# Transposes of one row chunk moved from TensorE to the DMA engines, with a reordered start and a split last tile

## The chip, the cores and the metric

The kernel runs on one NeuronCore of a Trainium2 chip. The metric is device time in microseconds (us); lower is better. Each kernel was run several times, each time beside runs of the kernel before on the same chip. The page and the traces come from the hardware profiler; their time zero is the start of the span, which is about 2 us shorter than the device time.

Engines are named as in the profile: PE is TensorE (matmuls), PEld its weight loads, DVE VectorE, ACT ScalarE, POOL GpSimd, SP SyncE. A "q" behind a name means the queue from which that engine issues DMA transfers. PSUM is the memory that PE writes to; the program has a pool `psum` of eight buffers of 128 x 512 f32 in it, called banks here.

## The reference, cut to what matters

```python
x = A_x                                          # [1, 2048, 1024] bf16
h = x + _A_ref(_layernorm(x), A_wqkv, A_wo)      # dilated local attention, 32 heads of 32
return h + _B_ref(_layernorm(h), B_w_gate, B_w_up, B_w_down)   # (x@w_gate * x@w_up) @ w_down
```

LayerNorm has no learned scale. `A_wqkv` is 1024 x 3072.

## The kernel before

The 2048 rows are worked through in four chunks of 512, each chunk in four tiles of 128 rows. A tile is normalized on DVE (`ln`, rows on partitions) and transposed (`lnT`, features on partitions), the layout in which PE's products here read it. The query-key-value product of a chunk is 24 groups of 8 matmuls. Each group fills one PSUM bank, which ScalarE copies to `sg`, and SyncE stores `sg` to DRAM in the layout that the attention reads back.

Chunk 0's transposes are on PE at the very start. Chunk 1's are on PE too, between matmul groups of chunk 0. Those of the other chunks are DMA transposes issued by SyncE.

```python
def stats(src, mv4, t):                   # DVE
    ...bn_stats of two halves, bn_aggr
def rstd_of(mv4, rs4, lo, hi):            # ScalarE: rs = exp(-0.5 ln(var + eps))
    nc.scalar.activation(rs4[:, lo:hi], mv4[:, lo:hi, 1], ACTF.Ln, bias=eps[:])
    nc.scalar.activation(rs4[:, lo:hi], rs4[:, lo:hi], ACTF.Exp, scale=-0.5)
...
    def transpose(self, t):
        ...
        nc.sync.dma_start_transpose(lnTs[c][:, :, bass.ts(t, 128)], self.lns[t][:])
    def transpose_on_array(self, t):
        ...
        for hf in range(2):
            pt = psum.tile([128, KO // 2, 128], BF, tag="mm", name=f"ptb{c}_{t}_{hf}")
            for kk in range(KO // 2):
                nc.tensor.transpose(pt[:, kk, :], self.lns[t][:, bass.ts(4 * hf + kk, 128)], ident[:])
            copy = nc.vector.tensor_copy if hf else nc.scalar.copy
            copy(lnTs[c][:, bass.ts(hf, 4), bass.ts(t, 128)], pt[:])
...
def evac_qkv(c, m, ps):
    sg = t1k.tile(...)
    nc.scalar.copy(sg[:, HB:HB + TC], ps[:])      # frees the bank of group m
    ...nc.sync.dma_start(<qd, kd or vd in DRAM>, <sg>)
...
qkv(0, range(1, 4))
load_qk(0)                                # GpSimd reads queries and keys of chunk 0 back (qD, kD)
bg.finish(rows2)
for t in range(4):
    norm1[2].transpose(t)                 # SyncE
xtiles[3] = load_x(3, "x", nc.sync)       # four 256 KB loads, SyncE
pump(6)
bg.add(stats_gen(norm1[3]), bg.now + 6.0) # statistics of chunk 3, 6 us later by the kernel's own count
start_attention(0)
qkv(1, range(4))
```

Work added to `bg` is emitted between matmul groups, by an estimate of time that the program keeps; so the *order* of instructions in each engine's queue is fixed when the kernel is built.

Of the kernel before, what the change touches and what calls it, by code (L numbers as in the profile page):

```python
# [78 lines left out]
def kernel(  # L79
# [11 lines left out]
    nc = tc.nc  # L91
# [114 lines left out]
    lnTs = {}  # L206
# [3 lines left out]
    class Norm1:  # L210
# [11 lines left out]
        def norm(self, t):  # L222
            self.lns[t] = normalize(xtiles[self.c][t], self.mv4, self.rs4, t)

        def transpose(self, t):
            c = self.c
            if c not in lnTs:
                lnTs[c] = lnTp.tile([128, KO, TC], BF, tag="lnT", name=f"lnT1_{c}")
            nc.sync.dma_start_transpose(lnTs[c][:, :, bass.ts(t, 128)], self.lns[t][:])

        def transpose_on_array(self, t):
            c = self.c
# [9 lines left out]
    def rows_gen(n, on_array):  # L242
        for t in range(6):
            if t < 4:
                n.stat(t)
                yield 1.5
            if 0 < t < 5:
                n.norm(t - 1)
                yield 0.55
            if t > 1 and on_array:  # L250
                n.transpose_on_array(t - 2)
                yield 0.45

    def stats_gen(n):
        for t in range(4):
# [16 lines left out]
    def load_x0(t):  # L272
        nc.sync.dma_start(x0[t][:], x[bass.ds(t * 128, 128), :])

    def load_w0(lo, n):
        nc.scalar.dma_start(w0[:, lo:lo + n, :], wqkv_v[:, lo:lo + n, 0:512])

    load_w0(0, 4)
    load_w0(4, 4)
    for t in range(4):  # L280
        load_x0(t)
    nc.scalar.preload_act_table_set("natural_log_exp_and_others")
    warm = t1k.tile([128, TC], BF, tag="t1k", name="warm")
    nc.vector.memset(warm[:], 0.0)
    eps = const.tile([128, 1], F32)
# [39 lines left out]
    def first_half(t, i):  # L325
        if i == 0:
            sts[t] = small.tile([128, 2, nc.vector.BN_STATS_DIM], F32, tag="st", name=f"st0_{t}")
        nc.vector.bn_stats(out=sts[t][:, i, :], in_=x0[t][:, bass.ts(i, 512)])

    def first_rstd(t):  # L330
        nc.vector.bn_aggr(out=mv0[:, t, :], in_=sts[t][:])
        rstd_of(mv0, rs0, t, t + 1)
# [3 lines left out]
    def first_norm(t):  # L336
        lns[t] = lnp.tile([128, D], BF, tag="ln", name=f"ln0_{t}")
        for i in range(2):
            cols = bass.ts(i, 512)
            nc.vector.tensor_scalar(lns[t][:, cols], x0[t][:, cols], mv0[:, t, 0:1], rs0[:, t:t + 1],  # L340
                                    ALU.subtract, ALU.mult)

    def first_transpose(t):
        for hf in range(2):
            pt = psum.tile([128, KO // 2, 128], BF, tag="mm", name=f"pt{t}_{hf}")
            for kk in range(KO // 2):
                nc.tensor.transpose(pt[:, kk, :], lns[t][:, bass.ts(4 * hf + kk, 128)], ident[:])
            nc.scalar.copy(lnTs[0][:, bass.ts(hf, 4), bass.ts(t, 128)], pt[:])

    def first_mm(t, kos):  # L350
        for ko in kos:
            for j in range(4):
                nc.tensor.matmul(ps0[j][:, bass.ts(t, 128)], lhsT=wts["qkv", 0][:, ko, bass.ts(j, 128)],  # L353
                                 rhs=lnTs[0][:, ko, bass.ts(t, 128)], start=(ko == 0), stop=(ko == KO - 1))
# [3 lines left out]
    first_half(0, 1)  # L358
    first_rstd(0)
    for t in range(4):  # L360
        if t < 3:
            first_half(t + 1, 0)
        first_norm(t)
        if t < 3:
            first_half(t + 1, 1)
        if t > 0:
            first_mm(t - 1, range(0, 6))
        first_transpose(t)
        if t > 0:
            first_mm(t - 1, range(6, 8))  # L370
        if t < 3:
            first_rstd(t + 1)
# [6 lines left out]
    xtiles[2] = load_x(2, "x", nc.sync)  # L379
    norm1 = {c: Norm1(c) for c in (1, 2, 3)}  # L380
    bg.add(rows_gen(norm1[1], True))
    rows2 = rows_gen(norm1[2], False)
    bg.add(rows2)
    for j in range(4):
# [374 lines left out]
    def f16(ap):  # L759
        return ap.bitcast(F16)  # L760
# [19 lines left out]
    def fcells(homes):  # L780
        return [f16(t[:, k, :]) for t in homes for k in range(NH)]

    def dprod(ps, q, lhs, rhs, fresh, lo=0, n=TC):
        for k in range(NP):
            nc.tensor.matmul(ps[:, bass.ds(lo, n)], lhsT=lhs[k][:, bass.ts(q, 128)], rhs=rhs[k][:, bass.ds(lo, n)],  # L785
                             start=(fresh and k == 0), stop=(k == NP - 1), skip_group_check=not fresh)

    def result(c, rows, t, hf, ps, sc, other, lo=0, n=TC):
        cols = bass.ds(hf * 512 + lo, n)
        nc.vector.scalar_tensor_tensor(rows[:, cols], ps[:, bass.ds(lo, n)], sc,  # L790
                                       rows[:, cols] if other is None else other[:, bass.ds(lo, n)], ALU.mult, ALU.add)
        nc.sync.dma_start(outf[bass.ds(c * TC + t * 128, 128), cols], rows[:, cols])
# [124 lines left out]
    hs2 = hss[2]  # L917
# [83 lines left out]
    down = {}  # L1001
# [28 lines left out]
    ps_x = [psum.tile([128, TC], F32, tag="mm", name=f"dx{q}") for q in range(4)]  # L1030
    ps_y = [psum.tile([128, TC], F32, tag="mm", name=f"dy{q}") for q in range(4)]
# [6 lines left out]
    for q in range(4):  # L1038
        dprod(ps_x[q], q, HA["11"], fcells(down["b11"]), True)
        if q == 1:  # L1040
            scale_h.total(ps_y[3])
            inv = const.tile([128, 1], F32, name="inv_hd")
            nc.vector.tensor_tensor(inv[:], scale_h.inv, scale_d.inv, ALU.mult)
            inv = inv[:]
# [3 lines left out]
    HF = {k: [f16(a) for a in HA[k]] for k in HA}  # L1048
# [17 lines left out]
    p5 = []  # L1066
# [21 lines left out]
    for q in range(4):  # L1088
        dprod(ps_x[q], q, HF["22"], fcells(down["b21"]), False)
        result(3, hs3[q], q, 0, ps_x[q], inv, None)  # L1090
    for q, lo, n in ((0, 0, 512), (1, 0, 512), (2, 0, 512), (3, 0, 256), (3, 256, 256)):
        dprod(ps_y[q], q, HF["12"], fcells(down["b22"]), False, lo, n)
        result(2, hs2[q], q, 1, ps_y[q], inv, p5[q], lo, n)


# [1 line left out]
_INS = ['A_x', 'A_wqkv', 'A_wo', 'B_x', 'B_w_gate', 'B_w_up', 'B_w_down']  # L1097
# [26 lines left out]
```

## Time and profile before

| what | value | from |
|---|---|---|
| time, median | 780.2 us (779.8 to 780.3, four runs) | runs beside the changed kernel |
| PE busy | 770.7 of 778.0 us | page, busy times |
| sum of PE's waits | 3.9 us, six entries | view of waits |
| `ptb` transposes on PE | 32, 1.79 us | chain of waits |
| x of chunk 3, first tile landed | 54.43 us | the trace's record of issues and landings |

The lines behind the rows stand in the prediction. To read the page: "busy" is time in which an engine has an instruction at work; the chain runs back from the last instruction, at each step to what released it.

### The profile page before, as it was taken

To read this page: it belongs to the slowest core of one execution; us is meant where nothing else is said; L and a number is where in the kernel's file an instruction comes from. 1 tells how busy PE (TensorE), PEld (TensorE's weight loads), DVE (VectorE), ACT (ScalarE), POOL (GpSimd) and SP (SyncE) were. 2 spreads that over 40 slices of the span, in tenths; PEclk is the share of its full clock that TensorE was granted. 3 is DMA by queue.
4 is the path that set the end of the run, shared out by engine and by line. 5 is a ranking of instruction groups with operands and counts; after the bars stand their busy time and mean duration, and the time that the engine had idled before them with its cause. 6 is when DMAs were issued, how large, how long until landed. Compare 5 with 4: busy or idle time off the path is not lost.

```text
span 778.0 us, 10494 instructions
## 1 busy us (share of the span) xinstructions
PE 770.7 (99%) x3707; PEld 355.2 (46%) x3707; DVE 614.8 (79%) x805; ACT 473.3 (61%) x1028; POOL 142.1 (18%) x152
## 2 busy tenths in 40 slices
PE   8999999999999999999999999999999999999997
PEld 6544444444444444444444444444444444444444
DVE  6619999999899998999989989985554444579762
ACT  4626544323576652966769799746777677788230
POOL 0000000010000200002000001008778677600000
PEclk9999999999999999999999999999999999999999
DMA  8999693895955869867645383734332323730001
GB/s 279 254 230 209 166 286 84 259 297 144 341 191 169 298 206 237 276 208 247 219 155 196 115 308 107 168 91 115 101 106 58 109 72 92 260 119 28 1 27 55
DMA packets 181605, 133.86 MB, mean 172 GB/s; under 512 B 79024, under 2 KB 174384, under 8 KB 179504
## 3 DMA queue, kind: packets, MB, share of 16 engines
q1 hardware_dynamic: 176912, 110.12, 49.6%
q0 software_dynamic: 3584, 22.02, 8.2%
q10 hardware_dynamic: 1056, 1.05, 0.4%
q8 instruction: 29, 0.48, 0.3%
q14 instruction: 24, 0.20, 0.1%
HBM read 104.86 MB, written 22.02 MB: 163 GB/s over the span
## 4 chain that ended last, share of the span: by engine, by line
PE 89%; DVE 9%; DMA 1%; issue 0%; ACT 0%; SPq 0%; DVEq 0%
PE ps L390 20%; PE pu L390 12%; PE pg L390 12%; PE dx L785 6%; PE pz L678 6%; PE acc L624 6%; PE py L678 6%; PE px L678 6%; PE wo L511 4%; PE pv L678 3%; PE dy L785 3%; DVE h L832 1%; PE ps L353 1%; PE ex L785 1%; DVE h L790 1%; DVE prodx L778 1%
## 5 line engine op out<-in xcount | busy, mean ns | idle before, releaser
L390 PE MATMUL ps<-lnT,w_qkv 128*128 128x512 bf16 x736 | 159.7, 379 | 0.0
L390 PEld LDWEIGHTS <-w_qkv 128*128 128x128 bf16 x736 | 71.8, 98 | 85.9
L390 PE MATMUL pg<-lnT,w_wg 128*128 128x512 bf16 x448 | 105.8, 379 | 0.0
L390 PE MATMUL pu<-lnT,w_wu 128*128 128x512 bf16 x448 | 105.8, 379 | 0.0
L304 ACT CAST sg<-ps 128x512 bf16<-128x512 f32 x96 | 54.7, 589 | 54.0 <-PE ps L390 50.6
L473 DVE TENSOR_TENSOR pv<-vD,at 128x4096 bf16<-128x4096 bf16 x32 | 72.5, 2287 | 0.3
L430 DVE TENSOR_TENSOR prod<-qD,kD 128x4096 bf16<-128x4096 bf16 x32 | 72.4, 2284 | 0.1
L678 PEld LDWEIGHTS <-sw 128*128 128x128 f16 x448 | 43.8, 98 | 54.1 <-issue 1.5
L390 PEld LDWEIGHTS <-w_wg 128*128 128x128 bf16 x448 | 43.8, 98 | 52.9
L390 PEld LDWEIGHTS <-w_wu 128*128 128x128 bf16 x448 | 43.8, 98 | 52.9
L594 ACT CAST us<-pu 128x512 bf16<-128x512 f32 x56 | 33.1, 592 | 41.0 <-PE pu L390 40.9
L678 PE MATMUL px<-lnT,ws 128*128 128x512 bf16 x224 | 55.2, 379 | 0.0
L678 PEld LDWEIGHTS <-ws 128*128 128x128 f16 x336 | 32.9, 98 | 39.6
L624 PE MATMUL acc<-w_wd,gs 128*128 128x512 bf16 x224 | 48.5, 379 | 0.0
L485 POOL DMA_DIRECT2D od<-oD x4 | 2.2, 542 | 252.4 <-DVE oD L483 162.5
L659 POOL TENSOR_TENSOR sw<-ws 128x512 f16<-128x512 f16 x26 | 30.0, 1153 | 85.3 <-PE py L678 78.1
L589 ACT CAST gs<-pg 128x512 bf16<-128x512 f32 x56 | 32.8, 586 | 11.3 <-PE pg L390 9.2
L185 ACT ACTIVATE rs<-mv,eps 128x1 f32<-128x1 f32 (+1 forms) x25 | 7.4, 297 | 49.9 <-DVE mv L182 47.6
L432 DVE TENSOR_TENSOR prod<-prod 128x4096 bf16<-128x4096 bf16 x16 | 36.6, 2289 | 0.3
L539 ACT ACTIVATE junkd<-w_wd 128x512 bf16<-128x512 bf16 x56 | 34.3, 613 | 0.0
L624 PEld LDWEIGHTS <-gs 128*128 128x128 bf16 x224 | 21.9, 98 | 26.4
L695 ACT COPY py<-px 128x512 f32<-128x512 f32 x28 | 16.0, 570 | 26.3 <-PE px L678 26.3
(304 smaller groups left out, 1399.2 us busy)
## 6 DMA issues: line engine op xcount, KB each, us to landing
w_wg<-in_B_w_gate_dram SPq DMA_DIRECT2D x14, 1024.0 KB, 6.7
w_wu<-in_B_w_up_dram SPq DMA_DIRECT2D x14, 1024.0 KB, 5.5
w_wd<-in_B_w_down_dram SPq DMA_DIRECT2D x8, 896.0 KB, 7.3
w_pair<-in_B_w_gate_dram SPq DMA_DIRECT2D x14, 512.0 KB, 4.1
w_pair<-in_B_w_up_dram SPq DMA_DIRECT2D x14, 512.0 KB, 5.3
w_wo<-in_A_wo_dram SPq DMA_DIRECT2D x6, 1024.0 KB, 8.2
w_qkv<-in_A_wqkv_dram SPq DMA_DIRECT2D x5, 1024.0 KB, 9.4
kd<-sg SPq DMA_DIRECT2D x32, 144.0 KB, 3.1
```

The lines of the kernel that those rows point to most:

```text
L304: nc.scalar.copy(sg[:, HB:HB + TC], ps[:])
L390: nc.tensor.matmul(ps[:], lhsT=wt[:, ko, bass.ts(j, 128)], rhs=rhs[:, ko, :], start=(ko == 0), stop=(ko == KO - 1))
L430: nc.vector.tensor_tensor(prod[:, j], qD[:], kD[:, :, o:o + SUB], ALU.mult)
L432: nc.vector.tensor_tensor(prod[:, :, 0:16], prod[:, :, 0:16], prod[:, :, 16:32], ALU.add)
L473: nc.vector.tensor_tensor(pv[:, j], vD[:, :, o:o + SUB], at[:, w, None, :].to_broadcast((128, DH, SUB)), ALU.mult)
L511: nc.tensor.matmul(ps[:], lhsT=oTs[c][:, kk, t, :], rhs=wts["wo", c, hf][:, kk, :], start=(kk == 0), stop=(kk == KO - 1))
L539: nc.scalar.activation(junk, src, ACTF.Abs, accum_out=self.l1[:, k:k + 1])
L589: nc.scalar.copy(gs[:], pg[:])
L594: nc.scalar.copy(us[:], pu[:])
L624: nc.tensor.matmul(acc[t][:], lhsT=hT[f][:, bass.ts(t, 128)], rhs=wts["wd", c, hf, b][:, j, :], start=(f == 0), stop=(f == NF - 1))
L678: nc.tensor.matmul(ps[:], lhsT=lhs[:, ko, :], rhs=rhs[:, ko, :], start=(fresh and ko == 0), stop=(ko == 3), skip_group_check=not fresh)
L785: nc.tensor.matmul(ps[:, bass.ds(lo, n)], lhsT=lhs[k][:, bass.ts(q, 128)], rhs=rhs[k][:, bass.ds(lo, n)], start=(fresh and k == 0), stop=( ...
```

## The change

Intent: take the 32 transposes of chunk 1 off the engine that bounds the kernel and give them to the DMA engines, issued by ScalarE; begin the first normalization before the next tile's statistics; and put the two halves of the last output tile in two PSUM banks, so that PE need not wait for DVE's read of the first half (0.58 us in the trace before).

```diff
-        def transpose(self, t):
+        def transpose(self, t, eng=nc.sync):
...
-            nc.sync.dma_start_transpose(lnTs[c][:, :, bass.ts(t, 128)], self.lns[t][:])
+            eng.dma_start_transpose(lnTs[c][:, :, bass.ts(t, 128)], self.lns[t][:])
...
             if t > 1 and on_array:
-                n.transpose_on_array(t - 2)
-                yield 0.45
+                n.transpose(t - 2, nc.scalar)
...
-    load_w0(0, 4)
-    load_w0(4, 4)
     for t in range(4):
         load_x0(t)
+    load_w0(0, 4)
     nc.scalar.preload_act_table_set("natural_log_exp_and_others")
+    load_w0(4, 4)
...
     for t in range(4):
-        if t < 3:
+        if 0 < t < 3:
             first_half(t + 1, 0)
         first_norm(t)
+        if t == 0:
+            first_half(1, 0)
...
-    for q, lo, n in ((0, 0, 512), (1, 0, 512), (2, 0, 512), (3, 0, 256), (3, 256, 256)):
-        dprod(ps_y[q], q, HF["12"], fcells(down["b22"]), False, lo, n)
-        result(2, hs2[q], q, 1, ps_y[q], inv, p5[q], lo, n)
+    for q in range(4):
+        ...            # q < 3 as before; behind q == 0:
+                nc.scalar.copy(ps_x[0][:, 256:512], ps_y[3][:, 256:512])
+        else:
+            for ps, lo in ((ps_y[3], 0), (ps_x[0], 256)):
+                dprod(ps, q, HF["12"], fcells(down["b22"]), False, lo, 256)
+                result(2, hs2[q], q, 1, ps, inv, p5[q], lo, 256)
```

More of the change, by code (lines that the diff above doesn't have):

```diff
@@ L1090 @@
         result(3, hs3[q], q, 0, ps_x[q], inv, None)
-    for q, lo, n in ((0, 0, 512), (1, 0, 512), (2, 0, 512), (3, 0, 256), (3, 256, 256)):
-        dprod(ps_y[q], q, HF["12"], fcells(down["b22"]), False, lo, n)
-        result(2, hs2[q], q, 1, ps_y[q], inv, p5[q], lo, n)
+    for q in range(4):
+        if q < 3:
+            dprod(ps_y[q], q, HF["12"], fcells(down["b22"]), False)
+            result(2, hs2[q], q, 1, ps_y[q], inv, p5[q])
+            if q == 0:
+                nc.scalar.copy(ps_x[0][:, 256:512], ps_y[3][:, 256:512])
[3 more added lines that the diff above has]
+                result(2, hs2[q], q, 1, ps, inv, p5[q], lo, 256)
 _INS = ['A_x', 'A_wqkv', 'A_wo', 'B_x', 'B_w_gate', 'B_w_up', 'B_w_down']
```

## The prediction

> **What bounds the kernel now.** I read the page first, then who TensorE (PE) waited for, the chain that ended last, the timelines of both ends, and the DMA issues with their landings.
>
> ```profile
> span 778.0 us, 10494 instructions
> PE 770.7 (99%) x3707; PEld 355.2 (46%) x3707; DVE 614.8 (79%) x805; ACT 473.3 (61%) x1028; POOL 142.1 (18%) x152
> PE 89%; DVE 9%; DMA 1%; issue 0%; ACT 0%; SPq 0%; DVEq 0%
> ```
>
> PE is busy for 99% of the span and holds 89% of the chain. A change can gain by taking instructions off PE, or by closing one of its few gaps. The view of PE's waits lists all of them:
>
> ```profile
> PE warm_ps L298 <- DVE warm L284: 1.2, 1, 1.2
> PE pv L678 <- DVE h L790: 0.9, 2, 0.7
> PE dy L785 <- DVE h L790: 0.6, 1, 0.6
> PE pt L347 <- DVE ln L340: 0.5, 1, 0.5
> PE ps L353 <- ACT lnT L348: 0.4, 1, 0.4
> PE dy L785 <- DVE prodx L778: 0.3, 1, 0.3
> ```
>
> The columns are total us, times, longest. The sum is 3.9 us. The change touches the third and fourth (the last tile; the first transpose) and adds no work to PE. So no result near the 2% line, 15.6 us, can come from gaps. The part taken off PE stands in the chain of the first 60 us:
>
> ```profile
> 17.29 6.91 PE ps L390 x32
> 24.20 0.45 PE ptb L238 x8
> 24.64 1.73 PE ps L390 x8
> 26.37 0.45 PE ptb L238 x8
> 26.82 1.73 PE ps L390 x8
> 28.54 0.89 PE ptb L238 x16
> 29.43 30.65 PE ps L390 x142
> ```
>
> The reader sees three groups of transposes of chunk 1 (ptb) wedged between matmul groups of 1.73 us, with no idle time around them.
>
> [...]
>
> [...] a transpose issued at 42.45 us, just before the 1152 KB load kD started (42.92), needed 5.4 us to land, the next two 9.1 and 8.5, against 3.2 us for quiet ones.
>
> [...] at the start the first weight half and two x tiles, the same 512 KB on two queues, land at 5.17 and 5.86 us.
>
> [...]
>
> [...] PE's second half of the last tile waits for the DVE read of other columns of that bank (next part).
>
> **Part 1: first tile normalized early.**
>
> ```profile
> 5.65 0.20 ACT L186 ACTIVATE rs<-rs 128x1 f32<-128x1 f32 x1
> 5.89 0.69 DVE L328 BATCH_NORM_STATS2 st<-x 128x6 f32<-128x512 bf16 x1 [0.60 <-DMA x<-in_A_x_dram]
> 6.50 0.72 DVE L340 TENSOR_SCALAR ln<-x,mv,rs 128x512 bf16<-128x512 bf16 x2
> 6.95 0.55 PEld L347 LDWEIGHTS <-ln 128*128 128x128 bf16 x8 [1.01 <-DVE ln L340]
> 8.35 0.31 ACT L185 ACTIVATE rs<-mv,eps 128x1 f32<-128x1 f32 x1
> 8.92 0.73 DVE L340 TENSOR_SCALAR ln<-x,mv,rs 128x512 bf16<-128x512 bf16 x2 [0.30 <-ACT rs L186]
> ```
>
> The scale of tile 0 is ready at 5.85, but DVE first does half a statistic of tile 1 (5.89 to 6.50). Reversed, the normalization starts at 5.89: 0.61 us earlier, so the first transpose moves from 6.95 to 6.34. That is not the gain. DVE does the same three pieces from 5.89, so tile 1's aggregate (at 7.85 for 0.21) stays. What moves is ScalarE: its copies of the first transposes (7.39 to 8.46) now end near 7.85, so tile 1's Ln starts when the aggregate is there, about 8.09 instead of 8.35. From there the loop transposes, copies, Ln/Exp, normalization repeats every 2.44 us (transposes at 9.39, 11.83, 14.27), which is also nearly PE's own work per tile. So 8.35 - 8.09 = 0.26 us is carried on. **Part 1: 0.26 us.**
>
> The order of loads in the diff should change nothing: ScalarE's queue works on its first 512 KB until 5.17. The second half, issued behind the 1.28 us table load (by about 3.1 instead of 1.24), is still in line by then and lands near 8.43 as before. It is needed for the fifth row block, at 7.41 + 16 x 0.06 = 8.4: just in time, and PE has spare time before the second transpose at 9.13.
>
> **Part 2: 32 transposes leave PE.** 0.45 + 0.45 + 0.89 = **1.79 us** of PE time (56 ns each), all on the path. Also gone are four DVE copies of 0.42 and four ScalarE copies of 0.59, all beside PE. Added are four DMA transposes issued by ScalarE. Their price is that of SyncE's:
>
> ```profile
> L229 SPq DMA_TRANSPOSE lnT<-ln x8: 1258/1280/5101, 41.0 to 94.2; - x8
> ```
>
> So about 1.28 us of ScalarE's time each, 5.1 in place of 4 x 0.59 = 2.4, and up to 5.1 us for one [...]. ScalarE is busy for 6.43 of 10 us in 15 to 25 and 4.19 of 6 us in 30 to 36; PE's next groups have spare PSUM banks of the 8. I expect late copies there but no stop of PE.
>
> **Part 3: last tile in two banks.**
>
> ```profile
> 772.34 0.48 DVE L790 SCALAR_TENSOR_TENSOR h<-dy,inv_hd,dp 128x256 bf16<-128x256 f32 x1 [0.78 <-PE dy L785]
> 772.88 0.81 PE L785 MATMUL dy<-dn_b22a,hq 128*128 128x256 f16 x6 [0.58 <-DVE h L790]
> ```
>
> The first half starts at 770.61 and has 14 matmuls at 0.108, so its last ends issue at 772.12; the second half starts only at 772.88, after DVE's read. In another bank it can start at once: 772.88 - 772.13 = **0.75 us**, and everything behind it (DVE 0.48, a store of about 1.6 us to landing) follows. The added ScalarE copy of the partial sum is emitted three products ahead, some 8 us before its use.
>
> **Sum:** 0.26 + 1.79 + 0.75 = 2.80 us; 780.2 - 2.8 = 777.4.
>
> **Does a shift of 2.05 us at 30 us survive to the end?** DVE is nearly full from 55 to 510 us, and the chain runs on it from 459 to 520. But its idle time near 205 (3.2 us), from 365 to 410 (5.4) and from 455 to 459 (2.2) ends at results of PE or of ScalarE copying PE's. So DVE can follow PE, and the 459 to 520 stretch starts earlier too. The tightest handover is the first output projection at 164.0 us, whose operand oT landed at 161.7: 2.3 us spare, 0.2 if PE alone moves. The attention feeding it starts after stores and loads that follow PE, so I expect it to move as well.
>
> **Rivals.**
> - *lnT of chunk 1 late.* It is first read when chunk 0's groups are through: 16.86 + 12 x 1.73 = 37.6 us. By the built order ScalarE issues the first transpose after the copy at about 24.5 and the other three in a row from about 27.7, so the last at 30 to 31.5. Quiet, they land 3.3 us later, at about 34. But the 1 MB load qD (issued 30.98, landed 36.89) runs then, and kD pushed such transposes to 9 us: then it lands at 37 to 39 and PE stops for 0 to 2 us. For it: DMA engines are 80% busy in 30 to 36. Against: one and a half of the four are through before qD's data flow. I give it one chance in three; the time would be 778 to 779.5.
> - *Attention follows late.* ScalarE's longer block delays the kd stores, so kD and DVE's start at 54.45; PE waits at the first output projection. Half of the gain would go: about 779. For it: the 2.3 us. Against: ScalarE has idle time to catch up by 40 us. One in ten.
> - *The start gives more.* If fewer bytes beside x bring tile 0 earlier than 3.73 us, all of the start moves: up to 0.6 us more, 776.8. Both queues are busy from the first byte in either order, so one in ten.
> - *A bound elsewhere swallows all* (780): the full-width idle points of DVE speak against it.
>
> **Range and chances.** With the first rival weighed in I say 777.6, a little above the bare sum. The low end, 776.8, is the sum plus a better start; the high end, 779.1, is a stop of 1.7 us. The three runs before lie within 0.43 us, so noise adds little. Both 2% lines are over 12 us away: chances 0.01, 0.98, 0.01.
>
> **What would show it.** Right: no ptb on PE and the matmul groups from 17 to 60 us unbroken; the first transpose near 6.3 but the second near 9.1; no wait of PE at the last tile's second half; PE's wait for prodx and h around 520 us still there, about 2 us earlier. Wrong: a PE gap near 37.6 us behind a DMA transpose; one at 162; the w_qkv load stopping the first matmuls at 8.4; ScalarE transposes of 4 us and more with PE short of banks; the last span of 774 to 778 not shortened.

The passages marked as cut said things of the hardware that no trace of this case shows: general rules beside the measured times, what was concluded from one of them about the transposes of two queues, and the reason given for the longest issue of a transpose. None is a term of the forecast's sum, which stands whole: 0.26 + 1.79 + 0.75 = 2.80 us.

## The result, and the profile after

The changed kernel takes 783.7 us (median of four runs, 782.0 to 784.9); the kernel before took 780.2 beside it. The ratio is 1.0045, with an interval of 1.0029 to 1.0061. By the 2% lines the two are "the same", as expected. But the predicted value was 777.6 with a range of 776.8 to 779.1: the sign was wrong, and the result is 6.1 us from it.

The page of the changed kernel, span, busy times (share of the span, instructions) and the chain by engine:

```profile
span 781.7 us, 10432 instructions
PE 770.4 (99%) x3675; PEld 353.7 (45%) x3675; DVE 613.6 (78%) x801; ACT 472.0 (60%) x1025; POOL 142.1 (18%) x152
PE 89%; DVE 4%; DMA 3%; ACT 1%; SPq 1%; ACTq 1%; issue 0%; DVEq 0%
```

PE has 32 instructions less (3675 for 3707), yet is busy for almost as long: 770.4 for 770.7 us. If 1.79 us of work is gone, other instructions must have become slower. And the span is 3.7 us longer, so there is also new idle time.

PE's waits after (total us, times, longest), the first two and two of the start:

```profile
PE ps L391 <- ACT sg L303: 3.4, 1, 3.4
PE pv L679 <- DVE h L791: 2.2, 2, 1.9
...
PE pt L346 <- DVE ln L339: 0.4, 1, 0.4
PE ps L352 <- DMA w_qkv<-in_A_wqkv_dram: 0.4, 1, 0.4
```

The first is new: PE stands still once, for 3.4 us, until ScalarE has copied a bank to `sg`. The second grew from 0.9 to 2.2. The wait of `dy` for `h`, 0.6 us at the last tile, is gone. A wait for the first weights is new.

**A ledger.** PE executes the same matmuls in both kernels, apart from the 32 transposes. So I matched them in order and read how much later each one starts. Where that difference steps, time was won or lost.

| where | step, us | what |
|---|---|---|
| start, up to the first full matmul group | +0.09 | 17.12 to 17.21 |
| chunk 1's transposes | -1.79 | as the chain before has it; the difference measured from 27.6 to 59 us is -1.70, with the start in it |
| 62.19 us | +3.53 | the stop for `sg` |
| just behind it | +1.69 | eight matmuls at half the clock, 0.21 us more each |
| around 520 us | +1.26 | PE's wait for `h`, 1.23 before, 2.49 after by matched starts |
| last tile | -0.74 | the second half need not wait |
| sum | +4.04 | spans differ by 3.7 |

The remaining 0.3 us lies after the last matmul: from the last store's landing to the end of the span it is 0.98 us in the changed kernel and 1.22 in the one before, which I take for jitter.

**What went as planned.** The timeline of the changed kernel at its last tile (start us, us, engine, line, operation, out<-in, count) has no idle time in brackets:

```profile
775.38 0.82 PE L786 MATMUL dy<-dn_b22a,hq 128*128 128x256 f16 x6
...
776.91 0.82 PE L786 MATMUL dx<-dn_b22a,hq 128*128 128x256 f16 x6
```

Before, the second half had waited 0.58 us for DVE. Now it stands in a bank of its own (`dx`) and follows at once.

**The stop.** First the kernel before, its timeline from 54 to 60 us. It shows nothing of a problem, but one must read it for what follows (in brackets stand the engine's idle time before the instruction and what ended it; PE's line is from a view of PE alone):

```profile
54.45 1.29 DVE L181 BATCH_NORM_STATS2 st<-x 128x6 f32<-128x512 bf16 x2 [16.17 <-DMA x<-in_A_x_dram]
...
56.02 0.29 ACT L185 ACTIVATE rs<-mv,eps 128x1 f32<-128x1 f32 x1 [8.69 <-DVE mv L182]
...
58.80 0.30 ACT L185 ACTIVATE rs<-mv,eps 128x1 f32<-128x1 f32 x1 [0.86 <-DVE mv L182]
...
59.24 0.57 ACT L304 CAST sg<-ps 128x512 bf16<-128x512 f32 x1
...
55.82 10.52 PE L390 MATMUL ps<-lnT,w_qkv 128*128 128x512 bf16 x48
```

The statistics of chunk 3 start when its x lands. ScalarE's queue holds the scales (`rs`) of three tiles, each waiting for DVE, and *behind* them the copy `sg`. Before the first of them ScalarE stands idle for 8.69 us and copies nothing, while PE fills the free banks. The copy ends at 59.81. The matmul group that reuses its bank starts at 60.35, so with 0.05 us for the signal (62.14 to 62.19 at the same handover in the changed kernel, below) there were 0.49 us to spare. PE runs through.

The same place after (PE's two lines again from a view of PE alone):

```profile
55.63 3.19 PE L391 MATMUL ps<-lnT,w_qkv 128*128 128x512 bf16 x14
56.78 1.29 DVE L181 BATCH_NORM_STATS2 st<-x 128x6 f32<-128x512 bf16 x2 [18.18 <-DMA x<-in_A_x_dram]
...
58.34 0.29 ACT L185 ACTIVATE rs<-mv,eps 128x1 f32<-128x1 f32 x1 [12.72 <-DVE mv L182]
...
61.13 0.30 ACT L185 ACTIVATE rs<-mv,eps 128x1 f32<-128x1 f32 x1 [0.86 <-DVE mv L182]
...
61.57 0.57 ACT L303 CAST sg<-ps 128x512 bf16<-128x512 f32 x1
...
62.19 8.11 PE L391 MATMUL ps<-lnT,w_qkv 128*128 128x512 bf16 x29 [3.37 <-ACT sg L303]
```

The order of the lines is the same, but everything that hangs on x is 2.33 us later, and ScalarE stands for 12.72 us in front of the first scale, while PE is 1.70 us earlier. 2.33 + 1.70 - 0.49 = 3.54 us: this is the stop. PE's gain of 1.7 us did not help here, it made the stop longer.

The granted clock of PE then falls. Windows of the changed kernel; the columns are the stretch, its length, busy time and count of PE, PEld, DVE, ACT and POOL, the granted clock, the share of the DMA engines and GB/s:

```profile
63.30:66.60 3.30, 3.30 (x9) 1.22 (x8) 3.30 (x2) 3.24 (x11) 0.00 (x0) 0.50 0.86 200
```

Half the clock for some 3.4 us: by the trace's clock records the slow stretch begins at 63.17 us, 1 us after PE restarted (62.19), and lasts 3.41 us. Before and behind it the granted clock is 1.00. This is why PE's busy time did not fall. The last section lists which other stops of PE had such a stretch behind them.

**Why x landed later.** The chain of waits of the changed kernel:

```profile
46.52 1.29 SPq L229
...
47.87 8.89 DMA x<-in_A_x_dram
56.78 1.30 DVE st L181 x2
```

x was *issued* earlier than before, at 47.87 instead of 50.37 us, but took 8.89 us to land instead of 4.06. So it was not the queue in front of x that was longer; the transfer itself was slow. Windows of the kernel before at the time of chunk 1's transposes, and then:

```profile
25.00:30.00 5.00, 5.00 (x43) 3.00 (x42) 3.66 (x10) 3.43 (x12) 0.00 (x0) 1.00 0.90 200
30.00:36.00 6.00, 6.00 (x30) 2.70 (x29) 5.90 (x13) 4.19 (x16) 0.70 (x1) 1.00 0.80 226
36.00:42.00 6.00, 6.00 (x29) 2.70 (x28) 1.35 (x4) 3.42 (x12) 0.00 (x0) 1.00 0.65 144
```

and the same windows after:

```profile
25.00:30.00 5.00, 5.00 (x25) 2.29 (x24) 3.31 (x7) 1.25 (x5) 0.00 (x0) 1.00 1.27 226
30.00:36.00 6.00, 6.00 (x30) 2.70 (x29) 2.35 (x6) 2.73 (x12) 0.70 (x1) 1.00 1.20 226
36.00:42.00 6.00, 6.00 (x29) 2.71 (x28) 2.39 (x6) 5.26 (x20) 0.00 (x0) 1.00 1.06 278
```

Look at the second column from the right, the DMA share. (It adds up the time of packets, so it can exceed 1, as the 1.27 here.) Before, the DMA engines had air: 0.90, 0.80, 0.65. After, they are full in all three, and from 36 to 42 us they move almost twice the bytes of before (278 GB/s for 144). Loads and stores slide back one behind the other: the last store of chunk 0's keys lands at 45.35 instead of 42.62, so the 1152 KB load kD starts at 46.17 instead of 42.92, and now runs against x.

Also ScalarE stood still, as the timeline of the changed kernel shows:

```profile
24.33 1.34 ACTq L229 DMA_TRANSPOSE lnT<-ln  x1
...
26.86 6.15 ACTq L229 DMA_TRANSPOSE lnT<-ln  x3
...
33.05 0.29 ACT L185 ACTIVATE rs<-mv,eps 128x1 f32<-128x1 f32 x1 [6.03 <-issue]
```

From 26.86 to 33.01 ScalarE did nothing but issue three transposes (1.32, 2.94 and 1.69 us). Its windows above show it: 1.25 us busy from 25 to 30, for 3.43 before. So there are two candidates for the late x: the *work* of the transposes on the DMA engines, and the *blocked ScalarE*, whose copies and stores come late. The experiments had to tell these apart.

**The wait at 520 us.** PE waits there for DVE (`h`), which in DVE's queue stands behind `prodx`. `prodx` reads the transposes of `lnr`; the last of the eight landed at 511.20 us before and 516.12 after, just ahead of its start at 511.48 and 516.25. SyncE issues these transposes behind four loads of weights (`w_pair`), the second at 499.51 and 504.51, as the third load lands (499.53 and 504.47). So late loads make late transposes, late products and a late PE. The view of those loads in the kernel before, for the stretch around the issue of the last two up-projection halves, and times from issue to landing:

```profile
L644 SPq DMA_DIRECT2D w_pair<-in_B_w_up_dram x2: 575/1138/1700, 492.4 to 494.1; - x2
DMA to landing us min/median/max: 3.9/5.5/7.2
```

and after:

```profile
L645 SPq DMA_DIRECT2D w_pair<-in_B_w_up_dram x2: 574/1892/3210, 496.0 to 497.7; - x2
DMA to landing us min/median/max: 5.5/7.0/8.3
```

The slowest took 8.3 us instead of 7.2. In this stretch hardly anything else is under way, but one thing is. The DMA view of the changed kernel from 498.5 to 499.2 us (packets, MB, share of 16 engines) has

```profile
q8 instruction: 1, 0.02, 10.1%
```

That is a 16 KB fetch of instructions. It is one packet. 10.1% of 16 engines over 0.7 us is 1.13 us, the time that it took (a view counts a packet where it starts). The slowest load is later by as much: 8.32 us for 7.21. There are 29 such fetches in a run, for 7414 instructions of PE and PEld in the kernel before: about one for every 256 (from the second fetch on, 218 to 289 start between one and the next). Without the 32 transposes PE has 64 instructions less (each with its weight load), so all later fetches come that much later in its program: this one at 498.7 us, inside the load, instead of 487.4, ahead of it.

### The profile page after: what moved, and what is told of

The parts are those of the page before. It is cut to its first block, busy times and chain, and to the rows that moved or that the text cites. A ratio compares the mean times of both kernels' runs of the same rounds, so it can differ in the third digit from the quotient of the medians.

```text
span 781.7 us, 10432 instructions
## 1 busy us (share of the span) xinstructions
PE 770.4 (99%) x3675; PEld 353.7 (45%) x3675; DVE 613.6 (78%) x801; ACT 472.0 (60%) x1025; POOL 142.1 (18%) x152
## 4 chain that ended last, share of the span: by engine, by line
PE 89%; DVE 4%; DMA 3%; ACT 1%; SPq 1%; ACTq 1%; issue 0%; DVEq 0%
PE ps L391 16%; PE pu L391 12%; PE pg L391 12%; PE dx L786 6%; PE pz L679 6%; PE acc L625 6%; PE py L679 6%; PE px L679 6%; PE wo L512 4%; PE wo L831 4%; PE pv L679 3%; PE dy L786 3%; PE ex L786 2%; DMA x<-in_A_x_dram 1%; DVE st L181 1%; DMA w_qkv<-in_A_wqkv_dram 1%
## 5 line engine op out<-in xcount | busy, mean ns | idle before, releaser
L679 PEld LDWEIGHTS <-ws 128*128 128x128 f16 x336 | 32.9, 98 | 39.6
L596 DVE TENSOR_TENSOR gs<-gs,us 128x512 bf16<-128x512 bf16 x56 | 23.5, 420 | 10.2 <-ACT us L595 10.2
```

What stands on the lines that cost most here:

```text
L679: nc.tensor.matmul(ps[:], lhsT=lhs[:, ko, :], rhs=rhs[:, ko, :], start=(fresh and ko == 0), stop=(ko == 3), skip_group_check=not fresh)
```

## The experiments

Theories, told in words here; the expectations give numbers for each. The loss comes (1) from ScalarE being blocked while it issues, so that its copies and stores come late; (2) from the changed start; (3) from PE merely running earlier into a queue that was slow anyway; (4) from the transposes' work on the DMA engines, which delays x of chunk 3. Theories on the wait at 520: the shifted instruction fetch, or anything else that follows the changed start and middle. Twelve kernels ran. Times are medians; the kernel before took 779.7, 779.9 and 779.95 in the three groups.

### e_dma: the transposes alone

The kernel before, with nothing but chunk 1's transposes moved.

```diff
-        def transpose(self, t):
+        def transpose(self, t, eng=nc.sync):
-            nc.sync.dma_start_transpose(lnTs[c][:, :, bass.ts(t, 128)], self.lns[t][:])
+            eng.dma_start_transpose(lnTs[c][:, :, bass.ts(t, 128)], self.lns[t][:])
-                n.transpose_on_array(t - 2)
-                yield 0.45
+                n.transpose(t - 2, nc.scalar)
```

> The kernel before with the DMA transposes on ScalarE's queue alone: old start, old last tile. Theory A (the four transposes block ScalarE for about 6 us from 27 to 33 us, the kd stores, the load kD and chunk 3's x come late, ScalarE stands before the scale of chunk 3 with PSUM copies behind it, and PE runs out of banks near 62 us): x lands at about 57 us, PE stops 3 to 3.6 us near 62, its clock drops for some 1.7 us, and the time is that of the changed kernel plus the 0.75 us of the last tile: 784 to 785 us. Rival B (the new order of loads and first tile makes everything late): no stop at 62 us, 778.0 to 778.8. The wait of PE for prodx near 525 us is about 2 us if it comes from where the instruction fetches fall, since PE has the same 64 instructions less.

Measured: 784.6 us (782.8 to 785.4), ratio 1.0058 (1.0042 to 1.0073). Its view of PE's waits:

```profile
PE ps L389 <- ACT sg L303: 3.1, 1, 3.1
```

x landed at 56.6, PE restarted at 62.04, and the clock dropped (0.50 from 62 to 64 us). The whole loss is in this one part of the change; the start is not its cause.

### e_skip: no transposes at all

The changed kernel, with each transpose replaced by two plain copies of `ln` into the place of `lnT` on DVE and ScalarE. The result is wrong (relative error 0.71), while PE has the same instructions as in the changed kernel and DVE and ScalarE the copies that they had before.

```diff
-                n.transpose(t - 2, nc.scalar)
+                n.fake(t - 2)        # nc.scalar.copy / nc.vector.tensor_copy, ln -> lnT, half each
+                yield 0.45
```

> The changed kernel with chunk 1's transposes replaced by plain copies of ln by DVE and ScalarE, wrong results on purpose: PE has the transposes off, but there are no DMA transposes and nothing blocks ScalarE. Theory A: x of chunk 3 lands before 55 us, PE's stop near 60 us is under 1.1 us, time 777.5 to 779.2. Rival C (PE being 1.8 us earlier is what runs it out of banks, whatever ScalarE and the DMA do): a stop of at least 2.5 us, 782 or more.

Measured: 778.35 us (778.0 to 779.0), ratio 0.9984. x landed at 51.7 us, and there is no stop at 60. The first line of its view of waits (the line of the changed kernel, for `sg`, is not in it):

```profile
PE pv L689 <- DVE h L801: 1.9, 2, 1.6
```

So theory 3 falls as the only cause: PE is as early as in the changed kernel (2.03 us ahead of the kernel before) and doesn't stop. It isn't free of blame: x landed 2.7 us earlier here than in the kernel before, so this run doesn't show the lead with x as it was. By the sum above that would be a stop of 1.70 - 0.49 = 1.2 us, an estimate. The wait at 520 us is long here too, without any DMA transpose: it has another cause.

### e_sp: the same transposes, issued by SyncE

```diff
-                n.transpose(t - 2, nc.scalar)
+                n.transpose(t - 2, nc.sync)
```

> The changed kernel with the same four DMA transposes issued by SyncE: same DMA work, ScalarE free. Theory A: ScalarE copies without a 6 us break, x of chunk 3 lands earlier than 56 us, PE's stop is 1.5 us or less, 777.5 to 780. Rival D (the 4 to 5 us of added DMA work delay x, whoever issues it): x lands at about 57 us and PE stops 3 us or more, 782.5 to 785.

Measured: 786.6 us (783.7 to 790.6), ratio 1.009 (1.0052 to 1.0129). ScalarE was free, as its window shows (3.40 us busy, for 1.25 in the changed kernel):

```profile
25.00:30.00 5.00, 5.00 (x25) 2.25 (x23) 3.31 (x7) 3.40 (x14) 0.00 (x0) 1.00 0.98 214
```

But x landed at 58.1, later still: here it was issued late, at 53.54 us behind the transposes in SyncE's queue, and landed 4.5 us after, so this run says nothing for theory 4. PE waited twice:

```profile
PE ps L391 <- ACT sg L303: 3.0, 1, 3.0
...
PE ps L391 <- DMA lnT<-ln: 1.6, 1, 1.6
```

Theory 1 falls as the only cause. The second line is the first rival of the prediction, `lnT` late: with SyncE issuing behind its stores it comes true, at 39.6 us. In the changed kernel it doesn't; the fourth transpose landed at 35.54 us, 2.4 us before PE began with chunk 1 (37.93).

### e_pool: DMA work without transposes and without a blocked engine

The kernel of e_skip, with each normalized tile also stored twice to a scratch tensor by GpSimd, which is otherwise idle but for issuing the loads qD and kD: 8 stores of 256 KB, 2.1 MB. Its output is wrong, which doesn't matter for the time.

```diff
                 n.fake(t - 2)
+                for r in range(2):
+                    nc.gpsimd.dma_start(scratch[r][t - 2], n.lns[t - 2][:])
                 yield 0.45
```

> The run without transposes again (plain copies, wrong results on purpose), with DMA work in their place that neither ScalarE nor SyncE issues: GpSimd stores each normalized tile twice into a scratch tensor, 8 x 256 KB, some 5 us of DMA work at the 390 GB/s of this stretch, in the same place of the program. Since the transposes from SyncE stopped PE as well, the blocked ScalarE is not the whole cause. Theory D (the DMA engines have little to spare between 20 and 57 us, so 4 to 5 us more work of any kind moves chunk 3's x by 4 to 5 us): x lands at 55.5 to 57.5 us instead of 51.7, PE stops 2.5 us or more, 781.5 to 785. Theory A' (a blocked issuing queue, ScalarE's or SyncE's, is what matters): x lands before 53.5 us, no stop over 1 us, 777.5 to 779.5.

Measured: 781.4 us (780.7 to 782.0), ratio 1.0022 (1.0005 to 1.0039), 3.1 us more than e_skip. The DMA engines moved 391 GB/s from 25 to 30 us. Its timeline:

```profile
60.81 1.46 PE L405 MATMUL ps<-lnT,w_qkv 128*128 128x512 bf16 x6 [2.02 <-ACT sg L317]
```

x landed at 54.5 instead of 51.7, the second tile at 56.8 instead of 53.5, the third at 57.3 instead of 55.6, and the stop is back, at the same place and for the same reason. Neither SyncE nor ScalarE had to issue anything more. The load qD went out at 36.05 us instead of 31.12, and what it waited for, by the timeline, was the landing of a `kd` store. So work on the DMA engines, without a blocked ScalarE, is enough to bring the stop; theory 4 is shown in kind. Its size is not: 2.0 us against 3.4, and the clock stayed at 1.00 from 54 to 68 us. These stores are somewhat less work than the transposes: between 24 and 60 us they raise GpSimd's queue from 20.7% to 36.0% of 16 engines, by 15.3 points, while the changed kernel's transposes make up 18.5%. The rest may be that, the blocked ScalarE, or which transfers happened to meet; these were not separated.

### e_late: the statistics queued later

If the stop comes from the place of the `rs` instructions in ScalarE's queue, it must go when they stand further back, with x as late as ever.

```diff
-    bg.add(stats_gen(norm1[3]), bg.now + 6.0)
+    bg.add(stats_gen(norm1[3]), bg.now + 14.0)
```

> The changed kernel with the statistics of chunk 3 put into the program 8 us later, so that ScalarE has copied five more groups before it stands before them. All theories of why x is late leave x late here (about 57 us). Theory A: PE has banks and does not stop near 62 us, its clock stays, and 3.5 + 1.7 us come back: 777.8 to 779.3. If PE waited for x or lnT itself, or for anything else than the copies behind the scale, it stops as before and the time stays at 782 to 785.

Measured: 779.0 us (778.65 to 779.5), ratio 0.999. The third tile of x landed at 57.3, yet PE runs through, as its timeline shows:

```profile
55.71 6.64 PE L391 MATMUL ps<-lnT,w_qkv 128*128 128x512 bf16 x30
```

The granted clock stays at 1.00 from 54 to 68 us. So the order in ScalarE's queue is a necessary part of the cause: late x alone costs PE nothing. (x was not quite as late as in the changed kernel: its first three tiles landed at 54.48, 56.69 and 57.30, for 56.76, 57.43 and 58.12 there. But e_pool, with 54.52, 56.78 and 57.30, stopped for 2.0 us; and with DVE's second statistic waiting for the second tile, 0.79 us later than in the kernel before, and PE 2.26 us ahead of it, the sum gives 0.79 + 2.26 - 0.49 = 2.6 us for the old order, an estimate.) There is a new wait later on, of 0.9 us for `ep` at 482 us, and the wait at 520 is 2.0.

### e_x3: x asked for earlier

The other way to cure it: leave the queue as it is and bring x early, by issuing its loads ahead of chunk 2's transposes.

```diff
+    xtiles[3] = load_x(3, "x", nc.sync)
     for t in range(4):
         norm1[2].transpose(t)
-    xtiles[3] = load_x(3, "x", nc.sync)
```

> The changed kernel with chunk 3's x loaded ahead of chunk 2's transposes on SyncE's queue. Four transposes of about 1.3 us and their wait on kD no longer stand before x, so it lands at 46 to 52 us instead of 56.8. If the late x is what holds ScalarE's copies, PE does not stop near 62 us: 777.8 to 779.3. If x is late for another cause than the queue ahead of it (the kd stores, say), it lands after 54 us and PE stops as in the changed kernel. Risk: chunk 2's transposes land 2 to 3 us later, but they are first needed at about 79 us.

Measured: 777.9 us (777.7 to 779.6), ratio 0.9979. x landed from 45.2 to 47.2 us, and there is no stop at 60. The wait at 520 is still 2.0 us. The fetch comes at 493.2 us and falls into the load there, which took 8.25 us.

### e_fetch: the instruction fetch put back, on e_late

PE gets 64 instructions more ahead of everything: 45 short warm-up matmuls in place of 13 long ones. The fetches should then fall at the same places of its program as in the kernel before.

```diff
-    for i in range(13):
-        nc.tensor.matmul(wps[:], lhsT=warm[:, 0:128], rhs=warm[:], start=True, stop=True)
+    for i in range(45):
+        nc.tensor.matmul(wps[:, 0:148], lhsT=warm[:, 0:128], rhs=warm[:, 0:148], start=True, stop=True)
```

> The run with late statistics, with 64 more instructions on PE: 45 warm-up matmuls of 148 columns for 13 of 512, the same columns in all, so that PE has as many instructions as before the change and its 16 KB instruction fetches fall near the same matmuls as before. If the wait for prodx near 520 us (0.8 + 0.4 us before, 2.0 in every kernel with 64 instructions less) comes from a fetch that falls into the load of w_pair, it goes back to about 1.2 us in all and the time falls by 0.8 to 1.3 us against 779.0: 777.6 to 778.3. If it comes from something else, PE being early say, it stays at 2.0 and the time at 778.6 to 779.5.

Measured: 785.0 us (784.8 to 785.2), ratio 1.0065. In part a miss. Its waits:

```profile
PE wo L831 <- ACT ep L929: 5.8, 1, 5.8
...
PE pv L679 <- DVE h L791: 0.9, 2, 0.6
```

The wait at 520 is back to 0.9, as expected of the fetch. But a wait of 0.9 us in e_late, for `ep` at 482 us, is 5.8 us now, and the mean granted clock of the run is 0.996, for 0.999 in e_late. The chain of waits there:

```profile
466.18 11.59 DMA lx<-in_B_w_down_dram
477.80 3.29 ACT lx L765
...
486.66 0.58 ACT ep L929
487.29 7.92 PE wo L831 x26
```

A load took 11.6 us, and ScalarE's work on it stands ahead of what PE needs. The store of the attention's result in front of it (`od<-oD`, 9.70 us) was not slower than elsewhere: 8.23 to 10.35 us in the other traces. Why the kernels with late statistics are late there is open: the later place of the statistics also changes DVE's order in the attention, but I did not test that. This kernel says that e_late's cure is fragile.

### e_tail: the last tile alone

```diff
-    for q, lo, n in ((0, 0, 512), ..., (3, 0, 256), (3, 256, 256)):
+    ...as in the change, on the kernel before
```

> The kernel before with the last tile in two banks and nothing else. The wait of 0.6 us for DVE at the last tile is gone, the second half starts 0.75 us earlier and nothing else moves: 779.0 to 779.5 us. If the added ScalarE copy delays the last products instead, no gain: 779.8 or more.

Measured: 779.3 us (778.9 to 779.9), ratio 0.9993. PE's wait for `h` at the last tile is gone. Against the kernel before of its group (779.9) the gain is 0.6 us, for 0.75 predicted.

### e_start: the start alone

```diff
-    load_w0(0, 4)
-    load_w0(4, 4)
     for t in range(4):
         load_x0(t)
+    load_w0(0, 4)
     ...and the normalization of tile 0 ahead of first_half(1, 0), as in the change
```

> The kernel before with the new order of loads and the first tile normalized early, nothing else. By the trace of the changed kernel the second half of the first weights lands at 8.4 to 9.0 us and takes back what the early tile gives, so 0 to 0.5 us: 779.4 to 780.3. If the start is worth its predicted 0.26 us the mean is 779.6 to 779.8, which this run can only just tell.

Measured: 779.8 us (779.6 to 780.1) against 779.95, ratio 0.9999. So the start is worth 0 to 0.2 us. From the landing of tile 0 to the first full matmul group it takes 13.26 us here, 13.39 in the kernel before: 0.1.

### e_x3_before: the new load order alone

The edit of e_x3 on the kernel before.

```diff
+    xtiles[3] = load_x(3, "x", nc.sync)
     for t in range(4):
         norm1[2].transpose(t)
-    xtiles[3] = load_x(3, "x", nc.sync)
```

> The kernel before with the new load order of x and nothing else. PE has no stop near 60 us to lose there, so loading x first should move nothing: 779.6 to 780.4. If it gains over 1 us by itself, the gain of the run with x first was not the removal of the changed kernel's stop.

Measured: 779.9 us (779.6 to 780.2), ratio 1.0. Early x does nothing by itself. It was not a bottleneck until the transposes came.

### e_x3_fetch and e_x3_array: both cures, and the transposes by themselves

e_x3 with the fetch put back (45 warm-up matmuls of 128 columns):

```diff
-    for i in range(13):
-        nc.tensor.matmul(wps[:], lhsT=warm[:, 0:128], rhs=warm[:], start=True, stop=True)
+    for i in range(45):
+        nc.tensor.matmul(wps[:, 0:128], lhsT=warm[:, 0:128], rhs=warm[:, 0:128], start=True, stop=True)
```

> The run with chunk 3's x loaded first (777.9 us), with 64 more instructions on PE in the warm-up (45 matmuls of 128 columns for 13 of 512). In the earlier try on top of the late statistics PE's wait for prodx near 520 us went from 2.0 back to 0.9 as expected, but a stop of 5.8 us at 481 us, behind a late load lx and its conversion on ScalarE, hid it in the time. Here the attention starts earlier, not later, so no stop at 481 is expected. If the fetch that falls into the w_pair load is the cause of the wait at 520: wait about 0.9 in all, time 776.4 to 777.3. If not: wait 2.0, 777.6 to 778.3.

And e_x3 with chunk 1's transposes left on PE, which has the same number of PE instructions as e_x3_fetch:

```diff
-                n.transpose(t - 2, nc.scalar)
+                n.transpose_on_array(t - 2)
+                yield 0.45
```

> The same load order with chunk 1's transposes left on TensorE: the new start and last tile, x first, no DMA transposes on ScalarE's queue. This is what the transposes are worth once the stop is gone. If PE's 1.79 us come through and only the fetch eats into them (0.9 to 1.2 us), this kernel is 0.6 to 0.9 us slower than x first with DMA transposes (777.9), so 778.5 to 778.9; if the transposes brought nothing even then, 777.9 or less.

Measured: e_x3_fetch 776.9 us (776.5 to 777.1, five runs), ratio 0.9961 (0.9946 to 0.9976): 3.1 us faster than the kernel before, and the best of all. Its page and its waits:

```profile
span 775.1 us, 10442 instructions
```

```profile
PE pv L679 <- DVE h L791: 0.9, 2, 0.7
```

The fetch comes at 484.7 us, ahead of the load, which takes 7.27 us again.

e_x3_array took 778.9 us (778.7 to 779.1), ratio 0.9987. The difference of the two, 2.0 us, is what moving the transposes off PE is worth where nothing takes it back.

The slowest of the four `w_pair` loads and the fetch, over the kernels where I read both:

| kernel | fetch at, us | inside the load | load, us |
|---|---|---|---|
| before | 487.4 | no | 7.21 |
| e_tail | 487.1 | no | 7.27 |
| e_x3_fetch | 484.7 | no | 7.27 |
| e_skip | 493.7 | yes | 8.20 |
| e_late | 494.0 | yes | 8.24 |
| e_x3 | 493.2 | yes | 8.25 |
| after | 498.7 | yes | 8.32 |
| e_pool | 495.8 | yes | 8.41 |

There is no overlap between the two groups. The other six traces fit: 7.18 to 7.30 us with the fetch outside (e_start, e_x3_before, e_x3_array, e_fetch), 8.45 and 8.54 with it inside (e_dma, e_sp). The load `lx` near 465 us shows the same: 8.15 to 8.62 us in the six traces with a fetch in its course, 6.74 to 7.08 in the others, save e_fetch (11.59); in e_pool (6.96) the fetch began 0.6 us before the landing. Together with the warm-up edit, which touches nothing but the warm-up and so the place of the fetches, this shows the cause of the longer wait at 520.

## Why the prediction was wrong

**The transposes' own worth: right.** 1.79 us were promised, the ledger has -1.79, the pair of kernels above 2.0.

**The last tile: right.** 0.75 predicted, 0.74 in the ledger, about 0.6 in the run alone.

**The start: its size was off.** 0.26 us predicted, about 0.1 measured from x's landing. The first transpose came at 6.55 us (6.34 predicted; x landed 0.19 later in that run), but the second at 9.49 instead of 9.13. The prediction had said that the second half of the first weights "lands near 8.43 as before"; it landed at 8.99, and PE, at the fifth row block, waited for it, the new line in the view of waits. "The order of loads in the diff should change nothing" was wrong by some 0.4 us there. Its picture of the queue was wrong too: the second half went out at 1.29 us, not behind the table load "by about 3.1". That x and both halves landed a little later (0.19, 0.24 and 0.56 us) is shown, why is not.

**The step that failed: "I expect late copies there but no stop of PE."** The reason given was the spare PSUM banks, and, in the second rival, that "ScalarE has idle time to catch up by 40 us". Both hold at 30 us: PE has no gap from there to 58.8. What the prediction never asked is which copy has the smallest margin over the whole stretch in which its effects run on. It was the copy at 59 us, behind three scales that wait for x, with 0.49 us. The prediction had the delay of stores and of kD in its second rival, and gave it one in ten, but looked for the price at the output projection at 162 us, where no stop came, and took it to be half of the gain. It cost 3.53 + 1.69 = 5.2 us at 62 us: a stop, lengthened by PE's own lead, and the clock behind it.

**A price that was not worked out: the DMA engines.** The prediction charged the transposes to ScalarE's queue at 1.28 us each, and looked at the DMA share only for `lnT` itself. On the page, the queue of ScalarE reads in the kernel before

```profile
q10 hardware_dynamic: 1056, 1.05, 0.4%
```

and after

```profile
q10 hardware_dynamic: 5280, 2.10, 1.2%
```

0.8% of 781.7 us is some 6 us of all 16 engines for 1.05 MB, in a stretch where the engines had less than that to spare: from the shares shown above, 0.90, 0.80 and 0.65 over 5, 6 and 6 us, the free time from 25 to 42 us was 0.5 + 1.2 + 2.1 = 3.8 us, an estimate. The overflow of some 2 us is the size of x's delay (2.33), though I would not read more than the order of magnitude into that.

**"PE's wait around 520 us still there, about 2 us earlier": wrong by 1.26 us.** It stayed and doubled, because fewer PE instructions moved an instruction fetch into a load. Nothing in the prediction looked at the fetches, though the page lists their queue.

**The first rival, `lnT` late: did not come true** in this kernel (landed at 35.54), did in e_sp. Nor did the transposes of the two queues overlap: SyncE's first was issued at 41.73.

What stays open: how the late x divides between the DMA engines' work and ScalarE's blocked queue (e_pool gave 2.0 us of stop with the first alone, the change 3.4 with both; but in e_late, also with both, x landed as in e_pool to 0.1 us, so the difference need not be ScalarE's), and why e_fetch is late at 466 us. The spread of the changed kernel, 782.0 to 784.9, is much wider than that of the kernel before. A part of it can be a second slow stretch: the profiled run, with one, has a mean granted clock of 0.998, as has the run of 782.0, and the other two, 783.9 and 784.9, have 0.996, as has e_dma with two. Each costs about 1.7 us. That is an estimate; no profile of these two runs is kept.

## What to carry to other kernels

Moving the transposes from a full PE to DMA had three bills here: the issuing engine's queue (three held ScalarE for 6.15 us), the DMA engines (18.5% of 16 from 24 to 60 us), and the transfers behind (chunk 3's x landed 2.33 us later). Before predicting such a move, add the work to the DMA share of that stretch, follow which loads slide back, and look for the smallest margin between a queue like ScalarE's and the buffers that PE needs (0.49 us here), along the whole slide and not only beside the change. PE's own lead shrinks such a margin too: here by 1.70 us. When a gain vanishes, asking for the sliding load a few instructions earlier may bring it back: here that one edit turned +3.5 us into -2.1, and repairing the place of the instruction fetch made it -3.1.

## What the traces of this case show of the hardware

- The issue of DMA transposes held the issuing engine: three in a row held ScalarE for 1.32, 2.94 and 1.69 us, 6.0 of 6.15 us, while in the kernel before the median from issue to landing was 3.3 us.
- Beside other transfers, the four transposes made up 18.5% of 16 engines' packet time from 24 to 60 us, 6.7 us for 1.05 MB.
- A 16 KB instruction fetch takes time of the same DMA engines (10.1% of 16 over 0.7 us in the changed kernel): one that fell into a load made it 8.2 to 8.5 us instead of 7.2 to 7.3, and PE's wait 1.2 us longer.
- The granted clock was halved behind some stops of PE and not behind others:

| run | stop of PE, us | ends at, us | granted clock behind it |
|---|---|---|---|
| after | 3.37 | 62.19 | 0.50 from 63.30 to 66.60 |
| e_dma | 3.12 | 62.04 | 0.50 from 62 to 64 |
| e_sp | 3.00 | 63.49 | 0.66 from 62 to 67, the end of the stop with it |
| e_pool | 2.02 | 60.81 | 1.00 from 54 to 68 |
| e_dma | 1.99 | 524.88 | 0.53 and 0.61, below |
| after | 1.94 | 525.04 | 1.00 from 522 to 530 |

The windows of e_dma behind its second stop:

```profile
526.00:528.00 2.00, 2.00 (x7) 0.76 (x6) 2.00 (x4) 1.26 (x2) 0.00 (x0) 0.53 0.33 112
528.00:530.00 2.00, 2.00 (x7) 0.70 (x6) 0.79 (x1) 0.69 (x1) 0.99 (x1) 0.61 0.60 145
```

So a stop of 2.0 us had half the clock behind it in one run (1.99) and the full clock in another (2.02). What decides between them is not shown here.
